# Pooled attention and two expert layers on one core: value products over six and nine key tiles, raw weights decoded in place, and a plan that keeps GpSimd's and VectorE's SBUF-only steps apart

## The chip, the cores and the metric

One core of a Trainium2 chip runs the whole program as one launch. The metric is the device time of one execution in microseconds (us); the kernel before took 1269.2 us, the median of three runs from 1268.52 to 1271.25 us.

## What is computed

For four batches of eight heads, queries are averaged over neighbouring rows, attended over 1152 keys, and the result goes through two feed-forward layers. All inputs are float64 on the host and arrive as raw 64-bit words.

```
q_pool = q.reshape(B, H, S // 2, 2, D).mean(axis=3)        # B, H, S, D = 4, 8, 1152, 64
scores = scale * q_pool @ k^T
attn   = softmax(scores)
x      = (attn @ v), heads side by side                     # 2304 x 512
h      = x @ w_in;  x = max(0.01 * h, h) @ w_out            # d_ff 2048
h      = max(x @ w1, x @ w2, x @ w3);  out = h @ w_out2     # d_ff 768
```

## The kernel before

**Work.** Two heads make a pair; 16 pairs n = 0 to 15, four to a batch (NP = 4). Each pair has two phases (ph 0 and 1): five query tiles of 128 rows, then four. A phase has nine key tiles of 128 keys (KT = 9). TensorE computes scores (`s`, `s_118` and so on), VectorE their row maxima (L352 to L362), ScalarE the exponentials (L355, L358, L363). TensorE then transposes the probabilities key tile by key tile (`pst`, and `psf` for the fifth tile), ScalarE copies each from PSUM into a tile `pt` (L405), VectorE the fifth (L412). A tile `pt` holds PG = 3 key tiles; pool `pt` has two of them.

**Value products.** `values(n, ph, gr)` multiplies one such tile with V: three key tiles by two heads, six float32 matmuls, in the trace twelve records, since a float32 product takes two. Each head uses 64 columns of the array (128x64 weights) and writes one half of the bank `pv`; all other products use 128x128 weights. After the third group `evac` takes the bank out. So a phase has three visits to `values`, 96 in the program. `follow` emits one at the second key tile of the next group, and tells the mixer how much TensorE time it stands for.

**Experts.** The feed-forward layers of batch b run in between the attention of batch b + 1; those of the last batch run alone at the end. The generator `experts` yields pieces of product (`m`, `o`), which the main loop mixes with attention by `RATIO`, `AHEAD` and `CHAIN`. Weights come in 56 chunks. In the first batch each chunk is decoded from the 64-bit words: a load into `wraw` (L610, three buffers), ScalarE on the high words (L620), VectorE on the low words (L623), VectorE joins both into a second tile `wmant` (L626, two buffers), ScalarE rounds it to the first half of `wsplit` (L641), GpSimd subtracts to get the second half (L642), and a store keeps the split chunk in DRAM (L650). Later batches load the split chunk (L664).

**What sets the order.** All instructions are first emitted, then `plan()` orders each engine's. It simulates the five engines with a cost for each instruction (lines 904 to 942), buffers of each pool included, and picks the instruction that can start first; it repeats this with due times from a backward pass and keeps the best order. Each order is then fixed by dependencies without semaphores: on the chip every engine takes its instructions in that order and waits only for data and buffers. Two costs matter here: 100 ns when TensorE goes into a value product and 215 ns when it leaves one:

```
if values_now != values_last:
    t += 100 if values_now else 215
```

Of the kernel before, what the change touches and what calls it, by code (L numbers as in the profile page):

```python
# [8 lines left out]
F32 = mybir.dt.float32  # L9
F32R = mybir.dt.float32r  # L10
I32 = mybir.dt.int32
# [3 lines left out]
ALU = mybir.AluOpType  # L15
# [8 lines left out]
def kernel(  # L24
# [23 lines left out]
    T = S // 2  # L48
    NP = H // 2
    KT = S // 128  # L50
# [8 lines left out]
    X0 = 320  # L59
# [3 lines left out]
    PG = 3  # L63
# [66 lines left out]
    def matmul(**kwargs):  # L130
        return on_pe(nc.tensor.matmul, **kwargs)
# [260 lines left out]
        nc.scalar.copy(out=rb[ph][:, 0:256], in_=ps[:, 0:256])  # L392

    pts = {}

    def probs_t(n, ph, kt):
        g = kt % PG
        if g == 0:
            pts[kt // PG] = pt_p.tile([128, PG, 2 * X0], F32, tag="pt", name="pt")
        w = (X0, T - X0)[ph]  # L400
        ps = bank("pst")
        for i in range(4):
            transpose(ps[:, i * 128:(i + 1) * 128], keys_of(ptl[n, ph, i], kt), ident)
        dst = pts[kt // PG][:, g, 0:2 * w].rearrange("p (j c) -> p j c", j=2)[:, :, 0:256]
        nc.scalar.copy(out=dst, in_=ps.rearrange("p (j c) -> p j c", j=2))  # L405

    def probs_m(n, gr):
        ps = bank("psf")
        for g in range(PG):
            transpose(ps[:, g * 128:(g + 1) * 128], keys_of(ptl[n, 0, 4], gr * PG + g), ident)  # L410
        dst = pts[gr].rearrange("p g (j c) -> p g j c", j=2)[:, :, :, 256:X0]
        nc.vector.tensor_copy(out=dst, in_=ps[:, 0:PG * 128].rearrange("p (g j c) -> p g j c", g=PG, j=2))  # L412

    KEYS = [*range(0, KT - 1, 2), *range(1, KT - 1, 2), KT - 1]
    marks = []
    pv = [None]

    def values(n, ph, gr):
        w = (X0, T - X0)[ph]
        pt = pts.pop(gr)  # L420
        if gr == 0:
            pv[0] = ps_v.tile([128, 512], F32, tag="v", name="pv")
        unit[0] += 1
        for g in range(PG):
            kt = gr * PG + g
            for j in range(2):
                mm = matmul(
                    out=pv[0][64 * j:64 * j + 64, 0:w],
                    lhsT=vss[n][:, j, KEYS[kt]],
                    rhs=pt[:, g, j * w:(j + 1) * w],  # L430
                    start=(kt == 0),
                    stop=(kt == KT - 1),
                )
        unit[0] += 1
        marks.append(mm.ins.name)

# [34 lines left out]
    def attention():  # L471
        npair = B * NP
        load_pair(0)
        for j in range(2):
            pool_q(0, j, j + 1)
            early_q(j)
            prep_k(0, j)
        for i in range(2):
            scores(0, 0, i)
            normalise(0, 0, i)  # L480
        for j in range(2):
            prep_q(0, j)
        load_v(0)
        load_pair(1)
        for n in range(1, NP):
            load_v(n)
        spare_tiles()
        for i in range(2, 5):
            scores(0, 0, i)
            normalise(0, 0, i)  # L490
        phases = [(n, ph) for n in range(npair) for ph in range(2)]
        todo = {}

        def at(slot, cost, f, *args):
            todo.setdefault(slot, []).append((f, args, cost))

        def now(slot):
            spent = 0
            for f, args, cost in todo.pop(slot, []):
                f(*args)  # L500
                spent += cost
            return spent

        for u, (n, ph) in enumerate(phases):
            s0 = u * KT
            if u + 1 < len(phases):
                nxt = phases[u + 1]
                k = len(tiles_of(nxt[1]))
                for i in range(k):
                    if nxt[0] < NP:  # L510
                        t = max(0, s0 + KT - EARLIER - 2 * (k - 1 - i))
                    else:
                        t = s0 + S_AT[nxt[1]][i]
                    at(t, QK * 6 * (1 + (i == 4)), scores, *nxt, i)
                    at(t + 1, 0, normalise, *nxt, i)
            if ph == 0 and n + 1 < npair:
                early = n + 1 < NP
                when = PREP_AT[0 if early else 1] if n else (2, 3, 4, 5)
                at(max(0, s0 + (-8 if early else 1)), 0, pool_q, n + 1)
                for j in range(2):  # L520
                    at(max(0, s0 + when[2 * j]), TR * 3, prep_q, n + 1, j)
                    at(max(0, s0 + when[2 * j + 1]), TR * 4, prep_k, n + 1, j)
                if n + 2 < npair:
                    at(max(0, s0 + (-2 if early else 15)), 0, load_pair, n + 2)
                if n + 1 >= NP:
                    at(s0 + 8, 0, load_v, n + 1)
            if n < FREE:
                at(s0 + 4, TR * 2, spread, n, ph)
        if wide:
            for c in range(PRE):  # L530
                at(6 + c * (2 * NP * KT - 8) // PRE, 0, predecode, c)

        late = []

        def follow():
            pn, pph, pgr = late.pop()
            values(pn, pph, pgr)
            if pgr == KT // PG - 1:
                last = pn % NP == NP - 1
                if pph == 0 and last:  # L540
                    yield "room"
                evac(pn, pph)
                if pph == 1 and last:
                    yield "batch"
            return PG * 4 * (X0, T - X0)[pph] / 2400 + 0.565

        for s in range(len(phases) * KT):
            n, ph = phases[s // KT]
            gr, g = divmod(s % KT, PG)
            done = 0  # L550
# [12 lines left out]
            c += now(s)  # L563
            done += c
            yield done, max(0, want - c)
            yield 0, None
            if g == PG - 1:
                late.append((n, ph, gr))
        yield from follow()
        assert not todo  # L570

# [30 lines left out]
    loaded = [0]  # L602
    early = []

    def decoded(src):

        raw = wr_p.tile([128, 512, 2], I32, tag="wr", bufs=3, name="wraw")
        load = nc.sync.dma_start(out=raw.rearrange("p (a f) w -> p a (f w)", a=src.shape[1]), in_=src)  # L610
        if len(early) < 2:
            early.append((load.ins.name, marks[GATE]))
            tc.add_manual_dep(
                load.ins, marks[GATE],
                mybir.DependencyInfo(mybir.DependencyClass.Sync, mybir.DependencyReason.DATA),
                reason="weights behind the first pair",
            )
        low, high = raw[:, :, 0], raw[:, :, 1]
        m = wr_p.tile([128, 512], I32, tag="wm", name="wmant")
        nc.scalar.activation(  # L620
            out=high.bitcast(F32), in_=high.bitcast(F32), func=ACTF.Prelu, scale=2.0 ** -112, alpha=2.0 ** 32
        )
        nc.vector.tensor_scalar(  # L623
            out=low, in0=low.bitcast(U32), scalar1=2.0 ** -29, scalar2=7.0, op0=ALU.mult, op1=ALU.min
        )
        nc.vector.scalar_tensor_tensor(  # L626
            out=m, in0=high, scalar=3, in1=low, op0=ALU.logical_shift_left, op1=ALU.bitwise_or
        )
        return m.bitcast(F32)

    stores = []

    def split_chunk(c):
        src = chunks[c]
        if wide:
            r = decoded(src)
        else:
            r = wr_p.tile([128, 512], F32, tag="wm", name="wmant")
            nc.sync.dma_start(out=r.rearrange("p (a f) -> p a f", a=src.shape[1]), in_=src)
        t = w_p.tile([128, 2, 512], F32R, tag="w", name="wsplit")  # L640
        nc.scalar.copy(out=t[:, 0], in_=r)  # L641
# [184 lines left out]
    def plan():  # L826
# [77 lines left out]
        for n, node in enumerate(nodes):  # L904
            busy = late = move = 0.0
            for i in node["ins"]:
# [32 lines left out]
                else:  # L939
                    late = 45 + 2.44 * cols  # L940
                    busy = late - 45
            node["busy"], node["late"], node["move"] = busy, late, move

        after = [[] for _ in nodes]
# [33 lines left out]
        def forward(prio):  # L978
# [12 lines left out]
            port = 0.0  # L991
            values_last = False
            for _ in range(count):
                best = None
                for e in ENGINES:
                    for n in pool[e]:
                        t = max(ready[n], free[e])
                        for x in need[n]:
                            group = slots[x][0]
                            if queue[group][heads[group]] != x or not rooms[group]:  # L1000
# [16 lines left out]
                if e == "PE":  # L1017
# [2 lines left out]
                        t += 100 if values_now else 215  # L1020
                    values_last = values_now
                begin[n] = t
                free[e] = t + node["busy"]
                end = t + node["late"]
                if node["move"]:
# [154 lines left out]
```

## Time and profile before

| | |
|---|---|
| runs | 1268.52, 1269.2, 1271.25 us |
| profiled execution | 1269.53 us, its span 1267.7 us |
| granted TensorE clock, mean | 0.996 |
| TensorE busy | 1235.2 us, 97% of the span |
| VectorE, ScalarE, GpSimd busy | 632.7, 633.7, 297.6 us |

The page gives the busy time of each engine, the chain of work that ended last, and the costliest groups of instructions with the idle time before them. PE is TensorE's matmuls, PEld its weight loads, DVE VectorE, ACT ScalarE, POOL GpSimd, SP the engine that issues the DMAs. A matmul's shown duration includes its way through the array, so two neighbours overlap; what a matmul costs is read from one start to the next.

### The profile page before, as it was taken

The page shows a single profiled execution, that of the slowest core. Times are in us where ns is not written, and L with a number is a line of the kernel's source. Part 1 is how long each engine was busy: PE and PEld are TensorE (multiplying, and loading weights), DVE is VectorE, ACT ScalarE, POOL GpSimd, SP SyncE. Part 2 cuts the span into 40 slices and gives each one's busy share as a digit, 9 for nine tenths or more (in the row PEclk, how much of TensorE's full clock was granted, in tenths as well). Part 3 has the DMA queues.
Part 4 walks back from the last instruction along what each step waited for, and adds up shares of the span by engine and source line. Part 5 has one row for each costly group of instructions (what it writes and reads, how often), then busy time and mean ns, then how long its engine had stood idle before and what let it go on. Part 6 is the DMA issues. An engine that isn't in the chain of part 4 may idle for free.

```text
span 1267.7 us, 19153 instructions
## 1 busy us (share of the span) xinstructions
PE 1235.2 (97%) x7392; PEld 1002.7 (79%) x7392; DVE 632.7 (50%) x1100; ACT 633.7 (50%) x1251; POOL 297.6 (23%) x265
## 2 busy tenths in 40 slices
PE   6899999999999999999999999999999999999998
PEld 5566777877878797777877887877877788888888
DVE  6867667566866636455554545464554211222110
ACT  6987867676666645454444545454543322112111
POOL 1111144445543411211211102111201022224110
PEclk9999999999999999999999999999999999999999
DMA  5523167768685644444354544344343353333433
GB/s 159 152 73 76 38 208 231 259 209 284 222 256 201 217 149 136 139 136 158 123 158 137 150 162 143 128 139 144 122 131 107 119 184 132 124 126 103 147 111 105
DMA packets 86902, 193.29 MB, mean 152 GB/s; under 512 B 11292, under 2 KB 41756, under 8 KB 86812
## 3 DMA queue, kind: packets, MB, share of 16 engines
q1 hardware_dynamic: 86812, 192.08, 48.2%
q8 instruction: 58, 0.95, 0.3%
q14 instruction: 32, 0.26, 0.1%
HBM read 146.80 MB, written 35.13 MB: 144 GB/s over the span
## 4 chain that ended last, share of the span: by engine, by line
PE 87%; DVE 5%; ACT 4%; issue 2%; DMA 2%; POOL 0%; SPq 0%; POOLq 0%; ACTq 0%; DVEq 0%
PE m L123 47%; PE s L123 11%; PE pv L123 10%; PE pst L123 9%; PE o L123 6%; PE psf L123 1%; DVE q L284 1%; PE psk L123 1%; DVE mx L352 1%; DVE kt L233 1%; DMA qspare<-qspare 1%; ACT pt L405 1%; PE psq L123 1%; DMA wraw<-in_moe_w_dram 1%; DVE mx L353 1%
## 5 line engine op out<-in xcount | busy, mean ns | idle before, releaser
L123 PE MATMUL m<-x,w 128*128 128x512 f32 x1224 | 304.5, 396 | 0.6 <-PE psk L123 0.6
L123 PEld LDWEIGHTS m<-x,w 128*128 128x128 f32 x1224 | 224.0, 188 | 45.2 <-issue 1.9
L405 ACT COPY pt<-pst 128x512 f32<-128x512 f32 x288 | 167.0, 587 | 148.4 <-PE pst L123 146.6
L362 DVE TENSOR_REDUCE mx<-s 128x1 f32<-128x1152 f32 x108 | 146.4, 1356 | 156.7 <-PE s L123 153.4
L363 ACT ACTIVATE p<-s,mx 128x1152 f32<-128x1152 f32 x108 | 132.0, 1222 | 127.4 <-DVE mx L362 127.0
L123 PE MATMUL s<-kt,q 128*128 128x384 f32 x832 | 185.0, 357 | 3.9 <-ACT p L355 2.4
L123 PEld LDWEIGHTS pst<-ident,p 128*128 128x128 f32 x1080 | 126.8, 141 | 61.7 <-issue 24.9
L123 PE MATMUL pst<-ident,p 128*128 128x128 f32 x1080 | 169.8, 278 | 5.5 <-ACT pt L405 3.0
L764 POOL TENSOR_TENSOR g<-t,g 128x512 fp32r<-128x512 f32 x64 | 84.0, 1312 | 371.1 <-DVE g L763 366.8
L123 PEld LDWEIGHTS s<-kt,q 128*128 128x128 f32 x832 | 142.6, 194 | 9.3 <-ACT p L355 3.1
L123 PE MATMUL m<-g,w 128*128 128x512 f32 x576 | 146.0, 397 | 0.0
L123 PE MATMUL pv<-pt,v 128*64 128x320 f32 (+1 forms) x1008 | 140.8, 414 | 0.0
L123 PEld LDWEIGHTS m<-g,w 128*128 128x128 f32 x576 | 104.7, 188 | 18.9
L123 PEld LDWEIGHTS pv<-pt,v 128*64 128x64 f32 x1008 | 64.9, 136 | 58.0 <-issue 23.1
L123 PE MATMUL m<-x,wsplit 128*128 128x512 f32 x408 | 105.0, 402 | 0.0
L762 ACT ACTIVATE t<-m 128x512 f32<-128x512 f32 x80 | 44.4, 555 | 112.9 <-PE m L123 112.2
L642 POOL TENSOR_TENSOR wsplit<-wmant,wsplit 128x512 fp32r<-128x512 f32 x56 | 74.7, 1334 | 73.8 <-ACT wsplit L641 67.9
L123 PEld LDWEIGHTS m<-x,wsplit 128*128 128x128 f32 x408 | 74.4, 189 | 14.6 <-issue 0.9
L792 DVE TENSOR_TENSOR t<-m,t 128x512 f32<-128x512 f32 (+1 forms) x60 | 38.1, 636 | 79.7 <-PE m L123 79.3
L702 POOL TENSOR_TENSOR y<-t,y 128x512 fp32r<-128x512 f32 x24 | 32.8, 1365 | 187.2 <-ACT y L701 187.2
L763 DVE CAST g<-t 128x512 fp32r<-128x512 f32 x64 | 27.4, 428 | 82.8 <-ACT t L762 82.5
L626 DVE SCALAR_TENSOR_TENSOR wmant<-wraw 128x512 int32<-128x512 int32 x56 | 51.5, 922 | 30.8 <-POOL wsplit L642 30.1
(116 smaller groups left out, 1491.1 us busy)
## 6 DMA issues: line engine op xcount, KB each, us to landing
w<-w SPq DMA_DIRECT2D x168, 512.0 KB
w<-wsplit SPq DMA_DIRECT2D x56, 512.0 KB
wraw<-in_moe_w_out_dram SPq DMA_DIRECT2D x22, 512.0 KB
wraw<-in_moe_w_dram SPq DMA_DIRECT2D x18, 512.0 KB
kraw<-in_k_dram SPq DMA_DIRECT2D x15, 576.0 KB
qraw<-in_q_dram SPq DMA_DIRECT2D x15, 576.0 KB
q<-q SPq DMA_DIRECT2D x52, 160.0 KB
wraw<-in_moe_w_in_dram SPq DMA_DIRECT2D x16, 512.0 KB
```

The costliest lines, as they stand in the source:

```text
L123: mm = f(*args, **kwargs)
L233: nc.vector.tensor_tensor(out=t[lo, c], in0=src, in1=t[hi, c], op=ALU.subtract)
L362: nc.vector.tensor_reduce(out=mx[:, 0:1], in_=ps[:, :, 0:SN], axis=AX.XY, op=ALU.max, negate=True)
L363: nc.scalar.activation(out=p[2], in_=ps[:, :, 0:SN], func=ACTF.Exp, bias=mx[:, 0:1], accum_out=rs[:, i:i + 1])
L405: nc.scalar.copy(out=dst, in_=ps.rearrange("p (j c) -> p j c", j=2))
L626: nc.vector.scalar_tensor_tensor(out=m, in0=high, scalar=3, in1=low, op0=ALU.logical_shift_left, op1=ALU.bitwise_or)
L642: nc.gpsimd.tensor_tensor(out=t[:, 1], in0=r, in1=t[:, 0], op=ALU.subtract)
L702: nc.gpsimd.tensor_tensor(out=t[:, 1], in0=src, in1=t[:, 0], op=ALU.subtract)
L762: nc.scalar.activation(out=t, in_=ps[:, 0:k.n], func=ACTF.Prelu, alpha=0.01)
L763: nc.vector.tensor_copy(out=gt[:, 0], in_=t)
L764: nc.gpsimd.tensor_tensor(out=gt[:, 1], in0=t, in1=gt[:, 0], op=ALU.subtract)
L792: nc.vector.tensor_tensor(out=t, in0=ps[:, 0:k.n], in1=t, op=ALU.max)
```

## The change

Four edits. (1) `values` takes a list of groups. For pairs 4 to 7 the first two groups of a phase go together (six key tiles) and the third alone; for pairs 8 to 15 all three go together (nine key tiles); pairs 0 to 3 stay as they were. (2) For pairs from 8 on every second `pt` tile is taken from the pool of raw weights, which is free by then (named `ptw`). (3) The raw weights are decoded in place: two tiles of 8 KB per partition are cut into four halves, each the place of one chunk; the joined words overwrite the low words, at a step of two words, and the tile `wmant` falls away. The fifth load of raw weights so waits for GpSimd's subtraction of the first chunk, where before the fourth waited for VectorE's join. (4) `plan()` lets no GpSimd or VectorE TensorTensor, TensorCopy or TensorScalarPtr without a PSUM operand start while another such one runs. This is in the plan's model of time alone; no wait is added to the program. The mixer's figure for a visit keeps 0.565 us for each visit, so a merged one counts less.

```
+    def pt_tile(n):
+        big[0] += 1
+        if long(n) and big[0] % 2:
+            t = wr_p.tile([128, 4, 512], F32, tag="wr", name="ptw").rearrange("p a c -> p (a c)")
+            return t[:, 0:PG * 2 * X0].rearrange("p (g c) -> p g c", g=PG)
+        return pt_p.tile([128, PG, 2 * X0], F32, tag="pt", name="pt")
...
-    def values(n, ph, gr):
+    def values(n, ph, grs):
...
-        for g in range(PG):
-            kt = gr * PG + g
-            for j in range(2):
-                mm = matmul(
...
+        for gr in grs:
+            pt = pts.pop((n, ph, gr))
+            for g in range(PG):
+                kt = gr * PG + g
+                for j in range(2):
+                    mm = matmul(
...
+        trios = []
+        LAST = ((0, 1, 2), (1, 2), (2,))
...
-            return PG * 4 * (X0, T - X0)[pph] / 2400 + 0.565
+            return len(grs) * PG * 4 * (X0, T - X0)[pph] / 2400 + 0.565
...
-                late.append((n, ph, gr))
+                trios.append(gr)
+                if gr in LAST[min(n // NP, 2)]:
+                    late.append((n, ph, trios[:]))
+                    trios.clear()
...
-        raw = wr_p.tile([128, 512, 2], I32, tag="wr", bufs=3, name="wraw")
+        if not raws_w:
+            raws_w.extend(wr_p.tile([128, 4, 512], I32, tag="wr", name="wraw") for _ in range(2))
+        k = turns_w[0] % 4
+        turns_w[0] += 1
+        raw = raws_w[k % 2][:, 2 * (k // 2):2 * (k // 2) + 2].rearrange("p a c -> p (a c)").rearrange("p (c w) -> p c w", w=2)
...
-        m = wr_p.tile([128, 512], I32, tag="wm", name="wmant")
...
-            out=m, in0=high, scalar=3, in1=low, op0=ALU.logical_shift_left, op1=ALU.bitwise_or
+            out=low, in0=high, scalar=3, in1=low, op0=ALU.logical_shift_left, op1=ALU.bitwise_or
...
+            inside = not any(slots[t][0][0].startswith("ps_") for t, _ in accesses(i.ins))
+            node["shut"] = node["e"] in ("DVE", "Pool") and inside and i.opcode in (
+                "TensorTensor", "TensorCopy", "TensorScalarPtr"
+            )
...
+                        if nodes[n]["shut"]:
+                            t = max(t, shut)
...
+                if node["shut"]:
+                    shut = t + node["late"] - 30
```

**Where instructions move.** TensorE in the last phase of pair 15, before (`o` is the last product of the experts, `pst` a transpose of four tiles of one key tile):

```order
L123 MATMUL pv<-pt,v 64x256 x6
L123 MATMUL pst<-ident,p 128x128 x4
L123 MATMUL o<-w,y 128x256 x18
L123 MATMUL pst<-ident,p 128x128 x4
L123 MATMUL o<-w,y 128x256 x18
L123 MATMUL pst<-ident,p 128x128 x4
L123 MATMUL pv<-pt,v 64x256 x6
```

and in the changed kernel, from the end of phase 0 on:

```order
L123 MATMUL pst<-ident,p 128x128 x8
L123 MATMUL pv<-ptw,v 64x320 x6
L123 MATMUL pv<-pt,v 64x320 x6
L123 MATMUL pv<-ptw,v 64x320 x6
L123 MATMUL pst<-ident,p 128x128 x24
L123 MATMUL o<-w,y 128x256 x15
L123 MATMUL pv<-pt,v 64x256 x6
L123 MATMUL pv<-ptw,v 64x256 x6
L123 MATMUL pv<-pt,v 64x256 x6
L123 MATMUL o<-w,y 128x256 x129
```

Three visits became one, and the transposes stand closer together. Over the program 56 visits are left of 96.

VectorE while pair 4 is prepared, shortly before the first experts begin, before (`wraw` and `wmant` are weights, `q_126` and `kt_1657` the queries and keys of the pair, `psf` the transposes that L412 takes out):

```order
L233 TENSOR_TENSOR kt_1656<-psk,kt_1656 64x512 x2
L626 SCALAR_TENSOR_TENSOR wmant<-wraw 128x512 x2
L284 SCALAR_TENSOR_TENSOR q_126<-psq,q_125 64x4x32
L284 SCALAR_TENSOR_TENSOR q_126<-psq,q_125 64x4x40
L284 SCALAR_TENSOR_TENSOR q_126<-psq,q_125 64x4x32
L362 TENSOR_REDUCE mx<-s 128x1
L284 SCALAR_TENSOR_TENSOR q_126<-psq,q_125 64x4x40
L233 TENSOR_TENSOR kt_1657<-psq,kt_1657 64x128
L412 COPY pt<-psf 128x6x64
```

and in the changed kernel:

```order
L362 TENSOR_REDUCE mx<-s 128x1
L284 SCALAR_TENSOR_TENSOR q_126<-psq,q_125 64x4x32
L284 SCALAR_TENSOR_TENSOR q_126<-psq,q_125 64x4x40
L284 SCALAR_TENSOR_TENSOR q_126<-psq,q_125 64x4x32
L284 SCALAR_TENSOR_TENSOR q_126<-psq,q_125 64x4x40
L233 TENSOR_TENSOR kt_1657<-psq,kt_1657 64x128
L423 COPY pt<-psf 128x6x64
L646 TENSOR_SCALAR wraw<-wraw 128x512
L649 SCALAR_TENSOR_TENSOR wraw<-wraw 128x512
```

The joins of the weights (L626, now L649) went from ahead of the copy of `psf` to behind it.

## Rows read from the trace of the kernel before

**Rows 1.** The page: busy time of each engine, and the chain that ended last.

```profile
PE 1235.2 (97%) x7392; PEld 1002.7 (79%) x7392; DVE 632.7 (50%) x1100; ACT 633.7 (50%) x1251; POOL 297.6 (23%) x265
PE 87%; DVE 5%; ACT 4%; issue 2%; DMA 2%; POOL 0%; SPq 0%; POOLq 0%; ACTq 0%; DVEq 0%
```

**Rows 2.** Windows by stage: width, busy us of each engine, clock, DMA share, GB/s.

```profile
0.00:180.00 180.00, 155.68 (x1011) 114.71 (x1012) 122.14 (x250) 140.70 (x327) 32.57 (x48) 0.98 0.40 118
180.00:445.00 265.00, 262.29 (x1493) 207.86 (x1492) 179.49 (x267) 180.93 (x337) 123.88 (x100) 0.99 0.71 229
445.00:1030.00 585.00, 584.35 (x3486) 471.43 (x3486) 285.80 (x503) 272.09 (x504) 88.51 (x67) 1.00 0.45 139
1030.00:1268.00 238.00, 232.88 (x1408) 208.65 (x1406) 45.27 (x80) 40.02 (x84) 52.63 (x52) 1.00 0.39 126
```

**Rows 3.** Timeline of PE, one visit of 256 columns, in narrow windows: start, us, work.

```profile
613.71 0.40 PE L123 MATMUL m<-g,w 128*128 128x512 f32 x1
...
614.30 0.60 PE L123 MATMUL pv<-pt,v 128*64 128x256 f32 x4
...
615.16 0.39 PE L123 MATMUL pv<-pt,v 128*64 128x256 f32 x2
...
615.64 0.38 PE L123 MATMUL pst<-ident,p 128*128 128x128 f32 x2
```

**Rows 4.** The same for other products: nine `m`, then four transposes.

```profile
619.18 2.25 PE L123 MATMUL m<-g,w 128*128 128x512 f32 x9
621.27 0.60 PE L123 MATMUL pst<-ident,p 128*128 128x128 f32 x4
```

**Rows 5.** Timeline of all engines around 158 us; in brackets idle time before, and its end.

```profile
155.21 1.28 POOL L642 TENSOR_TENSOR wsplit<-wmant,wsplit 128x512 fp32r<-128x512 f32 x1 [0.39 <-ACT wsplit L641]
...
155.47 2.18 DVE L626 SCALAR_TENSOR_TENSOR wmant<-wraw 128x512 int32<-128x512 int32 x2
...
155.90 1.29 PE L123 MATMUL s<-kt,q 128*128 128x384 f32 x6
...
160.93 0.54 DVE L412 COPY pt<-psf 128x384 f32<-128x384 f32 x1
161.06 1.12 PE L123 MATMUL psk<-ident,kraw 128*128 128x128 f32 x4 [2.83 <-DVE kt L233]
...
162.68 2.05 PE L123 MATMUL s<-kt,q 128*128 128x384 f32 x6
```

**Rows 6.** Tiles wraw and wmant: shortest, median, longest ns; then who waited for GpSimd.

```profile
L623 DVE TENSOR_SCALAR wraw<-wraw x56: 412/426/1522, 46.9 to 425.1; 128x512 int32<-128x512 uint32 x56
...
L626 DVE SCALAR_TENSOR_TENSOR wmant<-wraw x56: 661/693/1797, 47.4 to 431.7; 128x512 int32<-128x512 int32 x56
L641 ACT CAST wsplit<-wmant x56: 607/620/676, 152.3 to 448.2; 128x512 fp32r<-128x512 f32 x56
L642 POOL TENSOR_TENSOR wsplit<-wmant,wsplit x56: 1262/1292/1781, 153.6 to 448.9; 128x512 fp32r<-128x512 f32 x56
...
  DVE wmant L626: 30.1, 21
```

**Rows 7.** Chain of waits and timeline around 360 us.

```profile
353.43 7.61 DMA wraw<-in_moe_w_dram
...
359.95 0.63 PE L123 MATMUL psk<-ident,kraw 128*128 128x128 f32 x4 [0.86 <-DVE kt L233]
...
361.12 0.67 ACT L620 ACTIVATE wraw<-wraw 128x512 f32<-128x512 f32 x1 [2.02 <-DMA wraw<-in_moe_w_dram]
...
362.32 1.12 PE L123 MATMUL pst<-ident,p 128*128 128x128 f32 x4 [1.05 <-ACT pt L405]
```

**Rows 8.** Groups by line: count, busy us, mean ns, idle us before and its releaser.

```profile
L620 ACT ACTIVATE wraw<-wraw 128x512 f32<-128x512 f32 x56 | 38.3, 686 | 19.8 <-DMA wraw<-in_moe_w_out_dram 8.3 <-DMA wraw<-in_moe_w_in_dram 4.9 <-DMA wraw<-in_moe_w_dram 4.3
L405 ACT COPY pt<-pst 128x512 f32<-128x512 f32 x288 | 167.0, 587 | 148.4 <-PE pst L123 146.6 <-ACT p L363 0.2
...
L123 PE MATMUL m<-x,wsplit 128*128 128x512 f32 x408 | 105.0, 402 | 0.0
```

More of the change, by code (lines that the diff above doesn't have):

```diff
@@ L394, with long @@
     pts = {}
+    big = [0]
+    def long(n):
+        return n >= 2 * NP
+    def pt_tile(n):
[4 more added lines that the diff above has]
+        return pt_p.tile([128, PG, 2 * X0], F32, tag="pt", name="pt")
     def probs_t(n, ph, kt):
@@ L398, in probs_t @@
         if g == 0:
-            pts[kt // PG] = pt_p.tile([128, PG, 2 * X0], F32, tag="pt", name="pt")
+            pts[n, ph, kt // PG] = pt_tile(n)
         w = (X0, T - X0)[ph]
@@ L403, in probs_t @@
             transpose(ps[:, i * 128:(i + 1) * 128], keys_of(ptl[n, ph, i], kt), ident)
-        dst = pts[kt // PG][:, g, 0:2 * w].rearrange("p (j c) -> p j c", j=2)[:, :, 0:256]
+        dst = pts[n, ph, kt // PG][:, g, 0:2 * w].rearrange("p (j c) -> p j c", j=2)[:, :, 0:256]
         nc.scalar.copy(out=dst, in_=ps.rearrange("p (j c) -> p j c", j=2))
@@ L410, in probs_m @@
             transpose(ps[:, g * 128:(g + 1) * 128], keys_of(ptl[n, 0, 4], gr * PG + g), ident)
[L411 removed]
+        dst = pts[n, 0, gr].rearrange("p g (j c) -> p g j c", j=2)[:, :, :, 256:X0]
         nc.vector.tensor_copy(out=dst, in_=ps[:, 0:PG * 128].rearrange("p (g j c) -> p g j c", g=PG, j=2))
@@ L416 @@
     pv = [None]
-    def values(n, ph, gr):
+    def values(n, ph, grs):
         w = (X0, T - X0)[ph]
-        pt = pts.pop(gr)
-        if gr == 0:
+        if grs[0] == 0:
             pv[0] = ps_v.tile([128, 512], F32, tag="v", name="pv")
         unit[0] += 1
-        for g in range(PG):
-            kt = gr * PG + g
-            for j in range(2):
-                mm = matmul(
[L428 to L433, printed above, removed]
+        for gr in grs:
[4 more added lines that the diff above has]
+                    mm = matmul(
+                        out=pv[0][64 * j:64 * j + 64, 0:w],
+                        lhsT=vss[n][:, j, KEYS[kt]],
+                        rhs=pt[:, g, j * w:(j + 1) * w],
+                        start=(kt == 0),
+                        stop=(kt == KT - 1),
+                    )
         unit[0] += 1
@@ L533, in attention @@
         late = []
+        trios = []
+        LAST = ((0, 1, 2), (1, 2), (2,))
         def follow():
-            pn, pph, pgr = late.pop()
-            values(pn, pph, pgr)
-            if pgr == KT // PG - 1:
+            pn, pph, grs = late.pop()
+            values(pn, pph, grs)
+            if grs[-1] == KT // PG - 1:
                 last = pn % NP == NP - 1
@@ L603 @@
     early = []
+    raws_w = []
+    turns_w = [0]
     def decoded(src):
-        raw = wr_p.tile([128, 512, 2], I32, tag="wr", bufs=3, name="wraw")
+        if not raws_w:
[3 more added lines that the diff above has]
+        raw = raws_w[k % 2][:, 2 * (k // 2):2 * (k // 2) + 2].rearrange("p a c -> p (a c)").rearrange("p (c w) -> p c w", w=2)
         load = nc.sync.dma_start(out=raw.rearrange("p (a f) w -> p a (f w)", a=src.shape[1]), in_=src)
@@ L626, in decoded @@
         nc.vector.scalar_tensor_tensor(
-            out=m, in0=high, scalar=3, in1=low, op0=ALU.logical_shift_left, op1=ALU.bitwise_or
+            out=low, in0=high, scalar=3, in1=low, op0=ALU.logical_shift_left, op1=ALU.bitwise_or
         )
-        return m.bitcast(F32)
+        return low.bitcast(F32)
     stores = []
@@ L637, in split_chunk @@
         else:
-            r = wr_p.tile([128, 512], F32, tag="wm", name="wmant")
+            r = wr_p.tile([128, 4, 512], F32, tag="wr", name="wmant")[:, 0]
             nc.sync.dma_start(out=r.rearrange("p (a f) -> p a f", a=src.shape[1]), in_=src)
@@ L941, in plan @@
                     busy = late - 45
+            inside = not any(slots[t][0][0].startswith("ps_") for t, _ in accesses(i.ins))
+            node["shut"] = node["e"] in ("DVE", "Pool") and inside and i.opcode in (
+                "TensorTensor", "TensorCopy", "TensorScalarPtr"
+            )
             node["busy"], node["late"], node["move"] = busy, late, move
@@ L990, in forward @@
             held = [[] for _ in nodes]
-            port = 0.0
+            port = shut = 0.0
             values_last = False
```

## The prediction

> **What bounds the kernel now.** The page comes first: TensorE is busy for 1235.2 of 1267.7 us and makes 87% of the chain that ended last [rows 1]. A mean over 1268 us hides stages, so the windows come next [rows 2]. Up to 180 us, attention of the first batch alone, TensorE is without work for 180 - 155.7 = 24.3 us; here the other engines set the pace. From 180 to 445 us, where weights are decoded beside attention, it lacks 2.7 us, from there to 1030 us 0.7 us, and in the rest, which ends with the last store, 5.1 us. So from 180 us on, whatever TensorE doesn't have to do comes off the time nearly one for one, and what VectorE or GpSimd save there is worth nothing unless a wait of TensorE hangs on it. A busy TensorE is not one at its best, though, so I then read the starts of single products [rows 3, 4], and last the two places where it waited longest after the start-up [rows 5, 7].
>
> **Part 1: fewer visits to the value products.** The reader should see in [rows 3] that a visit costs more than its products. From the start of the `m` ahead of it to the start of the second transpose behind it, 615.64 - 613.71 = 1.93 us pass. What would the same work cost without a change of kind? One step of `m`: nine take 621.27 - 619.18 = 2.09 us [rows 4], 0.232 us each. Six pairs of value products (the two heads run side by side, so two records start together): from the second pair to the last, four steps take 615.16 - 614.30 = 0.86 us, 0.215 each, 1.29 for six. One step of a transpose: four show 0.60 us where one shows about 0.27 (the last's own way through the array: the two in [rows 3] show 0.38 with a step of 0.11), so (0.60 - 0.27) / 3 = 0.11 us. Together 0.23 + 1.29 + 0.11 = 1.63 us. The visit costs 1.93 - 1.63 = 0.30 us beyond its work. It lies at both edges, so I take it for 320 columns too.
>
> The order counts 96 visits before and 56 after. Pairs 4 to 7 save one in each of 8 phases, pairs 8 to 15 two in each of 16: 8 + 32 = 40, all of them in the stages in which TensorE is 99% busy [rows 2]. 40 x 0.30 = **12.0 us**. Ends of this term: if only half of the 0.30 were the edge and the rest moved elsewhere, 6 us; above 12 nothing in the rows reaches.
>
> What else the merging moves: a nine-tile visit is 18 pairs of 0.215 us, 3.9 us (more at 320 columns), in which ScalarE gets no transposes; and the transposes bunch up. The hardest spot is the x24 in the last phase. Six key tiles cost TensorE 24 x 0.11 = 2.6 us and ScalarE 6 x 0.587 = 3.5 us of copies [rows 8]. The difference of 0.9 us is covered by the 15 `o` products that stand ahead of the value products there. Without that cover it would be 0.9 us once. I take 0, with 0 and +0.9 for the ends. Every second tile comes from the weights' pool; GpSimd's last split starts at 448.9 us [rows 6], and pairs from 8 on belong to the stage behind. Cost 0. The smaller figure given to the mixer leaves more experts' work for the end of a batch (the x129), the same work in another place. Cost 0.
>
> **Part 2: the plan's order.** The longest wait of TensorE after the start-up is 2.83 us, ahead of `psk` at 161.06 [rows 5]. VectorE is its cause: two joins took 2.18 us, against 2 x 0.69 by their median [rows 6], while GpSimd subtracted from 155.21 on; behind them queued two query steps, a maximum, and the copy that frees the bank, at 160.93. After the wait TensorE was slow as well: `psk` 1.12 us against 0.63 for the same four [rows 7], six score products 2.05 against 1.29 [rows 5], which is its lower clock of 1.2 GHz (the mean granted up to 180 us is 0.98, [rows 2]). The place costs 2.83 + 0.49 + 0.76 = 4.1 us. In the changed order the decode steps stand behind that copy, so the 2.18 us leave the path. What is late next is the copy of transposes on ScalarE and the maximum ahead of it, so I don't take the whole: half, **2.0 us**. Ends: 0 and 4.1.
>
> The rows show that a join loses to GpSimd: median 0.69, longest 1.80 us, the difference 1.1 us a little under one subtraction of 1.29 [rows 6]. The Trainium skill, "SBUF — State Buffer", section "Who interferes with whom", says that a VectorE instruction with two SBUF inputs contends with a GpSimd instruction that reads SBUF, that the later one waits for the whole of the other, and that the order of issue decides who that is. By that rule a plan that sets only the order within each engine separates nothing on the chip, part 2 would be worth 0, and the sum 1257.5; by the moved rows it is 1255.5. The trace agrees as far as the one subtraction goes.
>
> The second place is at 360 us: 0.86 + 1.05 us of waits, then four transposes at 1.12 against 0.60 us, in all 2.4 us [rows 4, 7]. ScalarE sat behind a load of raw weights that took 7.61 us, with the copies of transposes queued behind it. In the changed kernel this load is still there, and the plan doesn't know its length. I take 0; ends -2.4 (gone) and +2.4 (a second one like it).
>
> **Part 3: decoding in place.** Load, decode and stores sit on SP, ScalarE, VectorE and GpSimd, none of which bounds this stage; products on fresh chunks waited 0.0 us [rows 8]. Three costs. VectorE and ScalarE now write or read at a step of two words. No row has the cast or the subtraction so; nearest is L620, 686 ns at that step, against 620 for L641 on plain rows: 66 x 56 = 3.7 us of ScalarE, which has 84 us free there [rows 2, 6, 8]. For GpSimd I bound it by 0 and by once more its 1.29 us, 72 us of the 141 it has free. Second, a place is held longer: load 7.61, L620 0.69, L623 1.52, L626 1.80, L641 0.68, L642 1.78, all at their longest [rows 6 to 8], 14.1 us. There are four, and a chunk comes every (448.9 - 153.6) / 55 = 5.4 us, so 21.5 us are to be had. Third, the fifth load waits for GpSimd where before the fourth waited for VectorE; queued behind it on SP are stores, query copies and key loads, each of which waited for that GpSimd step or for data of later use anyway. Against this, VectorE no longer waits for a free `wmant`, 30.1 us in 21 waits [rows 6], on no path of TensorE. Cost 0.
>
> **Sum.** The profiled execution took 1269.5 us (span 1267.7 and 1.8 around it), 0.3 above the median of the runs. 1269.5 - 12.0 - 2.0 = **1255.5 us**.
>
> **The rivals.** (a) *The plan's separation stays on paper.* The contention comes back in another place of the same length: part 2 gives 0, 1257.5 us. For it: no wait was added. Against: the joins really left the place of the longest wait. 17%. (b) *Both long waits go.* 1269.5 - 12.0 - 4.1 - 2.4 = 1251.0 us. For it: four loads are now under way early, and VectorE is freer. Against: the load's 7.61 us came from DMAs 71% busy in that stage [rows 2], and no transfer is removed. 10%. (c) *Long visits starve the others.* ScalarE gets nothing for 4 us, then TensorE waits for its copies. There are 24 merged visits, so at 0.5 us each the 12 us are gone: 1269.5 - 12 + 12 - 2 = 1267.5 us. Against: the plan puts `m` or `o` between, and its edge costs fit what [rows 3] give. 7%. (d) *In-place decoding runs dry*, the one that ends slower. Once a place is held for more than 21.5 us, each further us costs a quarter of it per chunk, 56 / 4 = 14 us. It decides from (12 + 2 + 2.5) / 14 = 1.2 us on, a hold of 22.7 us; at 23 us: 1255.5 + 21 = 1276.5 us. The queue on SP and a GpSimd that is twice as slow at that step speak for it, the 14.1 us at the longest rows against it. 4%. The forecast itself has 62%.
>
> **The numbers.** A measurement of this kernel can tell 0.2%, 2.5 us, from no change. Forecast, (a) and (b), 89%, are faster by far more, and a sixth of (c) too: 0.90. The rest of (c) is within it: 0.06. (d): 0.04. The range runs from (b) less a little to (c) half paid: 1250 to 1263 us; the 6 to 12 us of part 1 with no part 2 end at 1263.5.
>
> **What would show it.** Right: 56 visits, each again 0.30 us above its work; TensorE busy 12 us less from 180 us on, with the idle there unchanged at some 3 us; at the place of [rows 5] a wait under 1.5 us. (a) would show a wait of 2 us or more elsewhere before 180 us, with a VectorE step lengthened ahead of it; (b) idle below 1 us from 180 to 445; (c) waits of TensorE for L416 or for the value bank ahead of or behind merged visits; (d) `m` waiting for `wsplit`. Wrong altogether would be a stretch behind 445 us that isn't shorter: then the 0.30 us weren't the edge.

## The result, and the profile after

The changed kernel took **1250.1 us** (median of four runs, 1250.0 to 1251.2), the kernel before on the same chip 1270.2 us (four runs, 1268.5 to 1271.9): a ratio of 0.985, 95% interval 0.983 to 0.987. Forecast were 1255.5 us; against the profiled execution before, the gain is 19.4 us where 14.0 were expected. The time lies at the lower end of the range, on the figure of rival (b), 1251.0, but not for the reason that (b) gave.

The page of the changed kernel, busy times and chain, answers to [rows 1]:

```profile
PE 1220.3 (98%) x7392; PEld 1006.8 (81%) x7392; DVE 635.2 (51%) x1100; ACT 631.6 (51%) x1251; POOL 295.2 (24%) x265
PE 91%; ACT 4%; DVE 3%; issue 1%; DMA 1%; DVEq 0%; ACTq 0%
```

TensorE does the same 7392 records in 14.9 us less, and the time without work fell from 32.5 us (1267.7 - 1235.2) to 28.0 (1248.3 - 1220.3). The windows by stage, to hold against [rows 2] (columns as there):

```profile
0.00:180.00 180.00, 159.40 (x1037) 118.16 (x1037) 121.55 (x250) 142.56 (x328) 33.97 (x49) 0.98 0.41 118
180.00:445.00 265.00, 264.04 (x1555) 214.52 (x1554) 185.67 (x276) 188.00 (x350) 124.00 (x100) 1.00 0.74 234
445.00:1030.00 585.00, 582.55 (x3510) 482.02 (x3507) 287.33 (x502) 265.52 (x501) 92.71 (x73) 1.00 0.46 143
1030.00:1249.00 219.00, 214.28 (x1299) 192.05 (x1297) 40.66 (x72) 35.51 (x75) 44.49 (x44) 0.99 0.37 121
```

Without work were 20.6 us up to 180 (24.3 before), 1.0 up to 445 (2.7), 2.4 up to 1030 (0.7) and 4.0 in the rest of the span (4.8; the last window of either reaches past its end). Up to 445 us 2592 records are done against 2504 before. So the kernel gains early too, in stages where no or few visits are merged: 26 records up to 180 us, where pairs 0 to 3 kept their visits. From 180 us on TensorE is busy for 18.7 us less, of which it did 3.7 earlier (12 were forecast), and from 180 to 1030 us it lacks work for 3.4 us, as before (2.7 + 0.7). These are two of the signs that the forecast set for itself.

One visit of nine key tiles at 320 columns, timeline of TensorE in narrow windows, to hold against [rows 3]:

```profile
487.97 0.39 PE L123 MATMUL m<-g,w 128*128 128x512 f32 x1
...
488.29 0.49 PE L123 MATMUL pv<-ptw,v 128*64 128x320 f32 x2
...
492.92 0.44 PE L123 MATMUL pv<-ptw,v 128*64 128x320 f32 x2
493.29 0.33 PE L123 MATMUL pst<-ident,p 128*128 128x128 f32 x1
```

From the start of `m` the second transpose is 5.48 us away (it starts at 493.45 by its record). For the step of a pair I take all visits at 320 columns: from the first pair to the last those of three key tiles take 1.404 us, those of nine 4.634 (medians, worked out from the single records), 3.23 us for 12 steps more, 0.269 each. The work is then 0.23 + 18 x 0.269 + 0.11 = 5.18 us, by the working of part 1, and the visit costs 5.48 - 5.18 = 0.30 us beyond it. It isn't one lucky visit: of the visits at 320 columns that stand between an `m` and transposes and meet no wait, 24 of three key tiles before take 2.26 us from the start of `m` to that of the second transpose, five of nine here 5.48 (medians), again 3.22 us for the 12 steps. So nine key tiles pay no more at the edges than three.

The place of [rows 5] in the changed kernel, TensorE and VectorE, with two rows of GpSimd and ScalarE:

```profile
152.11 2.58 POOL L665 TENSOR_TENSOR wsplit<-wraw,wsplit 128x512 fp32r<-128x512 f32 x2 [1.14 <-PE psq L123]
...
154.99 0.55 PE L123 MATMUL psf<-ident,pend 128*128 128x128 f32 x3 [1.23 <-ACT pt L416]
...
155.40 1.23 ACT L363 ACTIVATE p<-s,mx 128x1152 f32<-128x1152 f32 x1
...
156.77 1.08 PE L123 MATMUL s<-kt,q 128*128 128x384 f32 x4 [1.24 <-ACT p L363]
...
157.60 0.70 DVE L649 SCALAR_TENSOR_TENSOR wraw<-wraw 128x512 int32<-128x512 int32 x1
157.66 1.05 PE L123 MATMUL psk<-ident,kraw 128*128 128x128 f32 x4
...
158.74 0.69 DVE L649 SCALAR_TENSOR_TENSOR wraw<-wraw 128x512 int32<-128x512 int32 x1
```

The joins run after these two subtractions and at their own length, 0.70 and 0.69 us. But TensorE waits here for ScalarE now, 1.23 and 1.24 us, and it still meets its lower clock of 1.2 GHz: the four `psk` take 1.05 us. Windows of this place (the clock is the third column from the right):

```profile
155.00:158.00 3.00, 1.76 (x9) 1.43 (x10) 2.82 (x8) 2.27 (x4) 0.00 (x0) 0.91 0.99 267
158.00:162.00 4.00, 4.00 (x22) 2.63 (x20) 3.06 (x5) 3.48 (x6) 2.91 (x3) 0.64 1.05 394
```

The lower clock takes 3 x 0.09 + 4 x 0.36 = 1.7 us; with the waits, 1.23 + 1.24 + 1.7 = 4.2 us. Before, the granted clock was 0.50 from 160.9 to 164.3 us, so by the same working the place cost 2.83 + 1.7 = 4.5 us; little of it is gone.

Around 360 us [rows 7] the window from 340 to 370, before and then after, shows that place gone but for 0.7 us; busy time rose from 28.09 to 29.27 of 30 us, and the clock from 0.94 to 1.00:

```profile
340.00:370.00 30.00, 28.09 (x158) 22.06 (x155) 21.47 (x34) 19.60 (x39) 11.70 (x10) 0.94 0.78 240
```

```profile
340.00:370.00 30.00, 29.27 (x165) 22.95 (x162) 22.76 (x36) 21.92 (x41) 14.13 (x12) 1.00 0.85 273
```

That is 1.2 us of idle time and 1.7 us of the lower clock (0.50 from 362.3 to 365.7 us before). The account of TensorE's 14.9 us is then 40 x 0.30 = 12.0 for the edges, 1.7 for this clock, and 1.2 that stay open.

Groups by line of VectorE's two decode steps before (busy, mean ns, idle before and its releaser):

```profile
L626 DVE SCALAR_TENSOR_TENSOR wmant<-wraw 128x512 int32<-128x512 int32 x56 | 51.5, 922 | 30.8 <-POOL wsplit L642 30.1
L623 DVE TENSOR_SCALAR wraw<-wraw 128x512 int32<-128x512 uint32 x56 | 33.3, 596 | 6.5 <-DMA wraw<-in_moe_w_out_dram 4.5 <-DMA wraw<-in_moe_w_in_dram 1.3 <-DMA wraw<-in_moe_w_dram 0.4
```

and of the decode steps after, which answer to these and to [rows 8]:

```profile
L665 POOL TENSOR_TENSOR wsplit<-wraw,wsplit 128x512 fp32r<-128x512 f32 x56 | 74.9, 1341 | 83.8 <-ACT wsplit L664 67.0 <-DMA wraw<-in_moe_w_out_dram 4.4 <-issue 3.6
L649 DVE SCALAR_TENSOR_TENSOR wraw<-wraw 128x512 int32<-128x512 int32 x56 | 45.9, 820 | 11.7 <-ACT wraw L643 8.2
L646 DVE TENSOR_SCALAR wraw<-wraw 128x512 int32<-128x512 uint32 x56 | 38.2, 682 | 0.4
L643 ACT ACTIVATE wraw<-wraw 128x512 f32<-128x512 f32 x56 | 38.6, 689 | 1.5 <-DMA wraw<-in_moe_w_out_dram 1.5
L664 ACT CAST wsplit<-wraw 128x512 fp32r<-128x512 f32 x56 | 37.4, 669 | 13.5 <-PE m L123 8.1 <-DVE mx L362 2.2 <-DVE wraw L649 1.4
```

Tile wsplit after, shortest, median and longest ns, to hold against [rows 6]:

```profile
L664 ACT CAST wsplit<-wraw x56: 641/668/721, 151.4 to 439.1; 128x512 fp32r<-128x512 f32 x56
L665 POOL TENSOR_TENSOR wsplit<-wraw,wsplit x56: 1294/1317/1760, 152.1 to 439.9; 128x512 fp32r<-128x512 f32 x56
```

The join's mean fell from 922 ns (L626) to 820, but that of the step ahead of it rose from 596 (L623) to 682 (L646): what the two lose to collisions is the same in both kernels. Over their undisturbed 694 and 426 ns it is 56 x (228 + 170) = 22.3 us before and 56 x (126 + 256) = 21.4 after. ScalarE's idle behind raw loads fell from 19.8 to 1.5 us.

### The profile page after: what moved, and what is told of

It reads as the page before. It is cut to its first block, busy times and chain, and to the rows that moved or that the text cites. A ratio compares the mean times of both kernels' runs of the same rounds, so it can differ in the third digit from the quotient of the medians.

```text
span 1248.3 us, 19152 instructions
## 1 busy us (share of the span) xinstructions
PE 1220.3 (98%) x7392; PEld 1006.8 (81%) x7392; DVE 635.2 (51%) x1100; ACT 631.6 (51%) x1251; POOL 295.2 (24%) x265
## 4 chain that ended last, share of the span: by engine, by line
PE 91%; ACT 4%; DVE 3%; issue 1%; DMA 1%; DVEq 0%; ACTq 0%
PE m L123 48%; PE s L123 13%; PE pv L123 11%; PE pst L123 10%; PE o L123 6%; PE psf L123 1%; PE psq L123 1%; PE psk L123 1%; ACT q L280 1%; DVE q L284 1%; DVE kt L233 1%; ACT kt L230 0%; ACT p L358 0%; ACT p L355 0%; ACT p L363 0%
## 5 line engine op out<-in xcount | busy, mean ns | idle before, releaser
L123 PE MATMUL pst<-ident,p 128*128 128x128 f32 x1080 | 166.4, 276 | 5.1 <-ACT pt L416 1.1
L416 ACT COPY pt<-pst 128x512 f32<-128x512 f32 x216 | 124.6, 587 | 82.6 <-PE pst L123 78.9
L123 PE MATMUL pv<-pt,v 128*64 128x256 f32 (+1 forms) x720 | 96.7, 407 | 0.0
L665 POOL TENSOR_TENSOR wsplit<-wraw,wsplit 128x512 fp32r<-128x512 f32 x56 | 74.9, 1341 | 83.8 <-ACT wsplit L664 67.0
L123 PEld LDWEIGHTS pv<-pt,v 128*64 128x64 f32 x720 | 48.5, 137 | 37.4 <-issue 8.8
L382 DVE TENSOR_SCALAR p<-p,sums 128x1152 f32<-128x1152 f32 x76 | 67.2, 885 | 2.6
```

Of the source, the lines that this page charges most:

```text
L123: mm = f(*args, **kwargs)
L382: nc.vector.tensor_scalar(out=x, in0=x, scalar1=rs[:, i:i + 1], scalar2=None, op0=ALU.mult)
L665: nc.gpsimd.tensor_tensor(out=t[:, 1], in0=r, in1=t[:, 0], op=ALU.subtract)
```

## The experiments

Twelve more kernels ran, each beside the kernel before, whose medians were 1269.4 to 1270.2 us. "Idle" is the window's width less TensorE's busy time in the one profiled execution.

| run | us | ratio, 95% | idle 0 to 180 | idle 180 to 445 | mean of a join, ns |
|---|---|---|---|---|---|
| before | 1270.2 | | 24.3 | 2.7 | 922 |
| after | 1250.1 | 0.985, 0.983 to 0.987 | 20.6 | 1.0 | 820 |
| e1_no_merge | 1263.1 | 0.996, 0.994 to 0.997 | 23.2 | 0.6 | 902 |
| e2_no_separation | 1269.4 | 1.000, 0.999 to 1.002 | 26.1 | 9.7 | 1058 |
| e3_separation_alone | 1263.9 | 0.996, 0.995 to 0.998 | 19.4 | 4.2 | 848 |
| e4_decode_alone | 1268.6 | 1.000, 0.998 to 1.001 | 23.1 | 3.3 | 1049 |
| e5_other_plan | 1250.9 | 0.985, 0.982 to 0.988 | 19.4 | 0.9 | 830 |
| e6_other_plan_no_separation | 1263.4 | 0.995, 0.993 to 0.997 | 22.7 | 8.1 | 1018 |
| e7_subtract_on_vector | 1260.3 | 0.992, 0.990 to 0.995 | 23.5 | 5.4 | 747 |
| e8_two_visits | 1254.8 | 0.988, 0.985 to 0.990 | 20.7 | 0.9 | |
| e9_join_priced_no_separation | 1264.0 | 0.995, 0.993 to 0.997 | 22.9 | 7.0 | 1089 |
| e10_join_priced | 1250.2 | 0.984, 0.982 to 0.986 | 20.8 | 0.7 | 856 |
| e11_first_batch_merged | 1253.4 | 0.988, 0.985 to 0.991 | 26.1 | 0.9 | |
| e12_subtract_on_vector_separated | 1251.3 | 0.985, 0.984 to 0.987 | 20.6 | 0.6 | 695 |

**The parts apart.** The first four take the change to pieces. e1 is the changed kernel with 96 visits again:

```
-        if long(n) and big[0] % 2:
+        if False:
-        LAST = ((0, 1, 2), (1, 2), (2,))
+        LAST = ((0, 1, 2), (0, 1, 2), (0, 1, 2))
```

> The changed kernel with three visits in every phase again (96 in all); decoding in place and the plan's separation stay. Theory A (the merging is worth its 40 edges of 0.30 us, the other 8 us of the 20 gained come from the plan and the decoding): 1250.1 + 12.0 = 1262 us. Rival B (the merging is worth all 20, as longer visits also leave other engines room): 1270 us. Rival C (the edges were mostly hidden, the plan's order made the gain): 1252 to 1255 us.

e2 is the changed kernel without the plan's separation:

```
-                        if nodes[n]["shut"]:
-                            t = max(t, shut)
```

> The changed kernel with a plan that lets GpSimd's and VectorE's SBUF-only steps start together; merging and decoding in place stay. If the separation in the plan brought the 8 us beyond the edges: 1258 us, with a long wait of TensorE again before 180 us. If it brought nothing (the steps still collide on the chip, 24.9 us of lengthened VectorE steps from 180 to 445 us in the changed kernel against 24.3 before): 1250 us.

e3 is the kernel before with the plan's lines on `shut` and nothing else of the change; e4 has both edits of e1 and e2, so only the decoding in place is left.

> The kernel before with the plan's separation and nothing else. If the separation brought the 8 us: 1262 us. If it works only together with the decoding or is worth nothing: 1270 us.

> The kernel before with decoding in place and nothing else. By my forecast it costs and brings nothing: 1270 us, TensorE idle from 180 to 445 us at 2 to 3 us. If four places held through the whole decode made the supply of weights steadier: 1264 to 1267 us, with the wait at 360 us and its slow clock gone.

Step by step the medians go from 1269.4 (before, in this set) over e4, 1268.6 (decoding in place: nothing that can be told), and e1, 1263.1 (separation: 5.6 us less), to 1250.1 (merging: 12.9 less). e3 gives separation 5.5 us by itself. In this order the parts are nearly what they should be, merging above all. In the other order they aren't: with no separation, merging is worth nothing, e4 to e2. e2's 1269.4 us lie far outside both times expected of it, 1258 and 1250. Its windows say where the gain went:

```profile
0.00:180.00 180.00, 153.88 (x1002) 112.86 (x1004) 124.56 (x246) 139.23 (x323) 32.44 (x47) 0.98 0.39 112
180.00:445.00 265.00, 255.29 (x1438) 204.00 (x1434) 189.59 (x266) 180.41 (x335) 122.17 (x97) 0.99 0.72 227
```

The edges are gone in e2 too (56 visits), but TensorE is without work for 9.7 us from 180 to 445 us, where e4 shows 3.3, and for 26.1 before that, against 23.1. Of the 19.3 us between e2 and the changed kernel, idle in these two windows makes 8.7 + 5.5 = 14.2. Around three long waits the granted clock also falls to 0.50 for 3.4 us each (from 168.5, 219.7 and 294.8 us), where the changed kernel shows one such stretch between 20 and 445 us: 2 x 1.7 = 3.4 us more. The waits of TensorE in e2 (total us, times, longest):

```profile
PE psq L123 <- ACT qraw L215: 6.4, 1, 6.4
PE pst L123 <- DVE kt L233: 5.3, 2, 4.1
PE m L123 <- DVE pt L423: 4.6, 1, 4.6
PE pst L123 <- DVE pt L423: 3.0, 2, 2.9
```

The first belongs to the start-up and stands in the changed kernel too, with 6.3; of the other three 1.2 us in all are left there, and no row of waits for VectorE is above 0.8 us. The longest of them, timeline of all engines in e2:

```profile
214.94 2.92 POOL L213 TENSOR_TENSOR qraw<-qraw 72x512 f32<-72x512 f32 x2 [0.17 <-PE psk L123]
...
215.24 1.50 DVE L646 TENSOR_SCALAR wraw<-wraw 128x512 int32<-128x512 uint32 x1
...
216.84 2.82 DVE L649 SCALAR_TENSOR_TENSOR wraw<-wraw 128x512 int32<-128x512 int32 x1
217.82 1.28 POOL L665 TENSOR_TENSOR wsplit<-wraw,wsplit 128x512 fp32r<-128x512 f32 x1
...
219.58 0.54 DVE L423 COPY pt<-psf 128x384 f32<-128x384 f32 x1
...
220.18 1.65 PE L123 MATMUL m<-g,wsplit 128*128 128x512 f32 x3 [4.56 <-DVE pt L423]
```

GpSimd works from 214.94 to 219.10 with hardly a gap: two additions of queries, then a subtraction. Beside them VectorE's L646 takes 1.50 us, where its median is 0.43, and the join 2.82 us, where alone it takes 0.69. Behind them in VectorE's order stands the copy that frees the bank `psf`, and TensorE stood for 4.56 us. This is the mechanism of [rows 5], longer. The Trainium skill, "SBUF — State Buffer", section "Who interferes with whom", has the later of two such instructions wait for the other. e2's rows agree as far as the second addition goes, which was under way when the join started. The subtraction started 0.98 us behind the join and still took its own 1.28 us, so the join lost to two GpSimd steps in a row, 2.1 us above its own length.

**Is it the order's luck?** The plan searches, so that any edit gives another order. e5 and e6 let it search from another cost of a semaphore, with and without separation:

```
-    SEM = 35
+    SEM = 45
```

> The changed kernel, but the plan reckons 45 ns for a semaphore in place of 35: another order on every engine, nothing else. If the 20 us rest on the edges and on the plan knowing the collisions, 1250 to 1254 us. If the plan's order is luck and the separation only threw other dice, anywhere from 1250 to 1262 us.

> The same other plan (45 ns) without the separation. If collisions of GpSimd and VectorE steps that the plan doesn't know cost the merged kernel its gain (e2), this one is slow again: 1262 to 1270 us, with single waits of TensorE of 2 us and more on VectorE before 300 us. If e2 was an unlucky order: 1250 to 1258 us.

A second thing was suspect: the plan's cost of a join goes by the name `wmant`, which the change does away with, so the join is planned too cheap. e9 and e10 price it as before, again without and with separation:

```
-                    slow = psum or op in ("TensorTensor", "TensorReduce") or kind == "wmant"
+                    slow = psum or op in ("TensorTensor", "TensorReduce") or (kind == "wraw" and len(list(accesses(i.ins))) > 1)
```

> As e2 (merged, decoded in place, no separation), but the plan reckons the join of the weights at the cost that it had before. The plan's rule goes by the tile that a step writes; since the join writes the raw weights in place, the changed kernel's plan takes it for the cheap kind, 0.35 us of VectorE where the trace shows 0.69. If this wrong price, and not the collisions, made e2 and e6 slow: 1250 to 1256 us. If the collisions did: 1262 to 1269 us, as e2 and e6. Half and half would be 1257 to 1261 us.

> The changed kernel with the join's price put right and nothing else. In the changed kernel TensorE sits without work for only 1 us from 180 to 445 us, so a better plan there has little to win: 1249 to 1251 us. If the wrong price still costs single waits before 180 us: 1247 to 1249 us.

With separation the three orders gave 1250.1, 1250.9 and 1250.2 us; without, 1269.4, 1263.4 and 1264.0. So luck moves the merged kernel without separation by 6 us, and separation is worth 12.5, 13.8 and 19.3 us in the three pairs. The unmerged kernel wasn't run with a second order, so its 5.5 us rest on e3 and on e4 to e1 alone. The price of the join doesn't matter when the steps are kept apart. When they aren't, it isn't the cause of what all three lose: e9 has the most costly joins of all, 1089 ns, and 7.0 us of idle from 180 to 445.

What separation changed on the chip can be worked out from the single records. Take TensorE's waits of over 0.3 us for VectorE from 20 to 445 us, and of these the ones with a VectorE step, in the wait or up to 4 us before it, that took over 0.1 us more than the median of its form. They come to 3.1 us in the kernel before, 2.8 in e4, 14.2 in e2, 5.7 in e6 and 7.2 in e9; with separation to 0 in e3, 0.6 in e1, 0.5 in the changed kernel, 0.4 in e5 and 0.6 in e10. The collisions themselves became fewer, but did not go: what L646 and L649 lose falls from 36.1 to 21.4 us from e2 to the changed kernel, and from 29.0 to 25.8 from e4 to e1. So what the plan changed most clearly is whether TensorE waits behind them. These waits are 13.7 of the 19.3 us from e2 to the changed kernel, but only 2.2 of the 5.6 from e4 to e1; what brought the rest there isn't shown.

**Is it the collision with the subtraction?** e7 takes the subtraction of the split away from GpSimd in e2, and e12 does so in the changed kernel:

```
-        nc.gpsimd.tensor_tensor(out=t[:, 1], in0=r, in1=t[:, 0], op=ALU.subtract)
+        nc.vector.tensor_tensor(out=t[:, 1], in0=r, in1=t[:, 0], op=ALU.subtract)
```

> As e2 (merged, decoded in place, no separation), but the 56 subtractions of the split run on VectorE and not on GpSimd. VectorE gets 56 steps of about 0.69 us more, 39 us, and 75 us of GpSimd's work in the stage from 180 to 445 us go, with most of what its steps can collide with. If the collisions cost e2 its 19 us: 1250 to 1257 us. If it was VectorE's load or the order as such: 1266 us or more.

> The changed kernel, separation and all, with the 56 subtractions of the split on VectorE: what is left of the collisions from 180 to 445 us (24.9 us of lengthened VectorE steps) mostly goes, for 39 us more of VectorE's own work. If those that are left cost TensorE nothing, as its 1 us without work there says: 1249 to 1252 us, no gain. If they still stretch the time somehow: 1245 to 1248 us. If VectorE becomes the one that is waited for: 1254 us or more.

Groups of e7, then of e12:

```profile
L665 DVE TENSOR_TENSOR wsplit<-wraw,wsplit 128x512 fp32r<-128x512 f32 x56 | 48.0, 860 | 12.8 <-ACT wsplit L664 11.7
L649 DVE SCALAR_TENSOR_TENSOR wraw<-wraw 128x512 int32<-128x512 int32 x56 | 41.8, 747 | 6.3 <-ACT wraw L643 2.0
```

```profile
L665 DVE TENSOR_TENSOR wsplit<-wraw,wsplit 128x512 fp32r<-128x512 f32 x56 | 46.1, 826 | 8.2 <-ACT wsplit L664 7.7
L649 DVE SCALAR_TENSOR_TENSOR wraw<-wraw 128x512 int32<-128x512 int32 x56 | 38.9, 695 | 4.8 <-ACT wraw L643 1.3
```

e7 came between the times expected of it: with the join at 747 ns, shorter than in the changed kernel, it took 1260.3 us, 10 more than the changed kernel. It is 9.1 us faster than e2, but only 3.1 and 3.7 faster than e6 and e9, the other orders without separation; with an order's luck of 6 us, the share of the collisions with the subtraction in e2's loss stays open. With the subtraction on VectorE and separation too, e12 took 1251.3, 9.0 less than e7, so separation does more than avoid these collisions. It could be the collisions with GpSimd's other steps (L213 above), or that SBUF-only steps which are held back let the copies that free a bank go first. No run tells these two apart, but the waits behind lengthened steps, counted as above, are only 2.2 us in e7 and 0.6 in e12. e12 also says that the collisions left in the changed kernel cost no more than the 46 us of added VectorE steps cost in their place.

**Doses of merging.** e8 gives pairs 8 to 15 two visits a phase instead of one (72 in all), e11 merges pairs 0 to 3 as well (48):

```
-        LAST = ((0, 1, 2), (1, 2), (2,))
+        LAST = ((0, 1, 2), (1, 2), (1, 2))
```

```
-        LAST = ((0, 1, 2), (1, 2), (2,))
+        LAST = ((1, 2), (1, 2), (2,))
```

> The changed kernel with two visits in each phase from pair 4 on (72 in all, not 56). Edges of 0.30 us on the path: 1250.1 + 16 x 0.30 = 1254.9 us. If a visit were worth more than its edges because long visits leave room elsewhere: 1257 us or more; if less: 1251 to 1252 us.

> The changed kernel with six key tiles to a visit in pairs 0 to 3 too (48 visits). There TensorE lacks work for 20 of 180 us, so if an edge is worth its 0.30 us only where TensorE is the bound, it brings less than 8 x 0.30 = 2.4 us: 1248.5 to 1250.5 us. With only two tiles for transposed probabilities it could also make TensorE wait there for ScalarE's copies: 1251 to 1254 us.

e8 took 4.7 us more than the changed kernel for 16 visits more, 0.29 each. Its waits of TensorE have one for a load, near 1007 us, which the changed kernel doesn't have:

```profile
PE o L123 <- DMA w<-w: 2.7, 1, 2.7
```

But it lacks the 2.3 us in which the changed kernel waits for VectorE and ScalarE behind 445 us. TensorE is idle for 28.3 us of e8's span and 28.0 of the changed kernel's, and busy for 4.5 us more, 0.28 for each visit: the fit is that of the edges.

e11 lost 3.3 us. Its waits of TensorE, beside its window up to 180 us, where idle is 26.1 against 20.6 us:

```profile
PE pst L123 <- ACT pt L416: 2.4, 2, 1.2
PE psq L123 <- ACT pt L416: 2.2, 3, 1.3
```

The changed kernel has 1.1 and 0.9 us in these rows. In the first batch there are only the two tiles `pt`; merged groups hold both, and ScalarE's copies then have nowhere to go: in e11 one of them waits 1.5 us for value products, in the changed kernel none does up to 180 us. This is rival (c), in the one stage that has neither a third tile nor experts' work to put between; the two rows are 2.6 of the 5.5 us of idle time that e11 has more there, and the rest isn't explained. The clock gave something back there: in e11 it stays at 1.00 from 150 to 170 us, where the changed kernel shows 0.91. Nothing that ran beat the changed kernel; e10 equals it.

## Why the prediction was too high

**Part 1 was right**, in size and in mechanism: 12.0 us forecast, 12.9 measured from e1 to the changed kernel, with the same edge of a visit at nine key tiles as at three. The stretch behind 445 us is 19.4 us shorter (822.7 to 803.3), the sign that was set for the edges; part of that is the 88 records done earlier, so e1 and e8 show it better. What it left unsaid is a condition: the 12 us come off the time only while no other engine is late. Without separation they came back as waits and as lower clock, all of them in e2; in e6 and e9 some 5 us of the 12 were left (1268.6 in e4 to 1263.4 and 1264.0). Why the merged order suffers more from collisions than the unmerged (e4 lost nothing against before) is argued, not shown: the merged order has TensorE through its work sooner and its transposes closer together, so that VectorE's late copies matter.

**Part 2 is the step that failed**, by its size and by its place. It took half of one wait of 4.1 us, 2.0 us, for the whole of separation; separation measured 5.5 us (e3, e4 to e1) and up to 19 with merging. The place named kept most of its cost, 4.2 us against 4.5: what was late next, ScalarE, took the wait, with the lower clock behind it. The sign set for (a), a wait of 2 us or more before 180 us behind a lengthened VectorE step, isn't there: the joins at that place run at 0.70 us. The gain lies elsewhere. TensorE's idle time fell by 3.7 us before 180 us, and the second place at 360 us, taken at 0 between -2.4 and +2.4, is worth 2.9 (1.2 of idle, 1.7 of clock). Neither is separation's alone. Idle before 180 us is 19.4 us in e3, but 23.2 in e1 against 23.1 in e4, where separation shows from 180 to 445 us instead (0.6 against 3.3; their profiled executions lie 2.5 us apart, not 5.6). At 360 us e3 keeps a wait of 1.05 us and e4 one of 1.43, both at full clock; with both edits, in e1, TensorE is busy for 29.99 of the 30 us. So where separation's 5.5 us fall differs from order to order. The prediction had no term for that, nor for what a collision costs once visits are merged; the sum came within 5.4 us because part 1 makes most of it.

**Rival (a)'s rule fell.** It said that a plan that sets only the order within each engine separates nothing on the chip. The collisions are what the rows took them for, but the plan's order, with the waits for data between the engines, keeps some of them apart: the join's mean is 1049 to 902 ns from e4 to e1, 1058 to 820 from e2 to the changed kernel, while the step ahead of it gives part of that back from e4 to e1 (589 to 679). The groups by line gave an upper bound, 22.3 us of VectorE for the two steps before. It is no price: e1 loses 25.8 and is 6.3 us faster, and e12, where they lose 3.4, is no faster than the changed kernel. The nearer figure was TensorE's waits behind lengthened steps, 3.1 us before, with the lower clock behind the longest.

**Part 3, decoding in place, was right** at 0: 1268.6 against 1269.4 us, no difference that can be told, and (d) never came near. Its inner costs were bounded well: by the medians, ScalarE's cast went from 620 to 668 ns on the step of two words, GpSimd's subtraction from 1292 to 1317. It took ScalarE's 19.8 us behind raw loads away (0.6 in e4); e4's joins are longer, 1049 ns instead of 922, but that the one paid for the other isn't shown.

**The sign for (b)**, idle below 1 us from 180 to 445, came about (0.96), and the time is (b)'s too, in part by luck. Its reason was half right: of its two long waits one went, and smaller ones made up for the other.

## What to carry to other kernels

The sum of what instructions of a kind lose (mean less undisturbed length, times the count) bounds what an edit on all of them can bring, but isn't its price: e1 loses 25.8 us that way, the kernel before 22.3, and yet e1 is 6.3 us faster. Look for the waits of the bounding engine behind the lengthened instructions, and for the lower clock behind long waits. Parts of a change needn't add up: fewer visits on the bounding engine paid 12.9 us with the other engines kept in time, and nothing to 5 us without, so each part is to be tried both alone and on top of the others. And where a planner chooses the order, try two or three orders of each variant before a difference of 6 us is put down to the edit.

## What the runs showed of the chip that was not expected

A VectorE step on SBUF can lose to two GpSimd steps in a row, the second of which starts after it: the join took 2.82 us in e2 against 0.69 alone, and the step on one input ahead of it (L646) 1.50 against 0.43. The edges of a value visit cost the same, 0.30 us, whether it has three key tiles or nine. A step of two words costs ScalarE's cast 48 ns on 512 columns (620 to 668 in median) and GpSimd's subtraction 25 (1292 to 1317).
